# Scale and K in chunks of 4 and 5 k-tiles, with the ones put into PSUM ahead of them, in a diffusion transformer block

## The chip, the cores and the metric

The kernel runs on one core of a Trainium2 chip. The metric is the device time of one execution in microseconds (us). Six executions of the kernel before took 247.53 to 249.71 us, their median is 249.35 us. The profile is of one execution: its own time is 247.53 us, the lowest of the six, and the stretch that the profiler covers (the span) is 245.4 us of it. About 2.1 us lie around the span.

## The reference

The kernel computes one block of a diffusion transformer for 2 batches of 256 tokens, D = 1152, two heads, and a hidden layer of 4608. All inputs are bf16.

```
mod = (silu(c) @ w_mod).reshape(B, 6, 1, D)
shift_a, scale_a, gate_a, shift_m, scale_m, gate_m = mod[:, 0..5]
h   = layernorm(x) * (1 + scale_a) + shift_a
q, k, v = split(h @ wqkv)
a   = softmax(q @ k.T * Dh ** -0.5) @ v @ wo
x   = x + gate_a * a
h2  = layernorm(x) * (1 + scale_m) + shift_m
out = x + gate_m * (gelu(h2 @ w_fc1) @ w_fc2)
```

What matters here is the start: the normalised x is multiplied by `1 + scale_a`, and K is taken from that product before shift_a is added. The shift adds the same term to every key of a batch, so that it drops out of the softmax; Q and V are taken from the product with the shift.

## The kernel before

D is cut into nine tiles of 128 ("k-tiles"), the 512 tokens into four token tiles, two for each batch. The head of the kernel goes as follows.

1. SP's queue loads x (two DMAs, one for each batch), then the scale columns of w_mod (WSC) for the first KC = 5 k-tiles in three DMAs of 480 KB (line 699), then the first five row tiles of the K weights (WK, 288 KB each, line 702), then WSC for the other four k-tiles, the other four of WK, and then the shift columns (WSH, three DMAs of 864 KB, line 704). These loads wait for nothing. After them come the Q weights (WQ), which take WSC's place in SBUF and so wait until WSC has been read.
2. silu(c) is made on ScalarE and VectorE (lines 721 to 727), while TensorE runs 16 dummy matmuls of 512 columns (`warm_a`, line 716, and `warm`, line 773).
3. LayerNorm's statistics of token tiles 1 and 2 are taken on VectorE (`ln_stats_dve`), of 0 and 3 on ScalarE by two sums (`ln_stats_act`); the power of -1/2 is GpSimd's. VectorE normalises each tile (`xn_*`, line 756), TensorE transposes it into PSUM (`xn_T`, line 763).
4. TensorE makes scale_a as columns: for each of the k-tiles of the contraction and each output k-tile of the chunk one matmul with 2 columns (`mod_kt`, line 778), accumulated in bank 7. `sc1a` (line 784) adds 1 on the way from PSUM to SBUF. `hk` (line 789) multiplies a transposed k-tile by that column, which gives HK. For k-tiles of the first chunk it reads PSUM; the others are first copied to HX (`xn_T_copy`, line 769).
5. TensorE makes K for batch 0 (four pairs of output tiles, banks 0 to 3) and batch 1 (three pairs, banks 5, 4, 6) with `k_pair` (line 807), k-tile after k-tile: the first chunk's k-tiles for batch 0, one pair of chunk and batch 1, then scale for the second chunk (36 matmuls with 2 columns), then the rest.
6. TensorE makes shift_a as rows ("shr", line 879: nine k-tiles of the contraction, each with four matmuls side by side in the array, of 384, 256, 256 and 256 columns), the last K pairs, Q, attention and the rest of the block. From here on the order is not touched by the change.

The order is set so: every operation is put down as a unit with an engine, a duration, and its reads and writes (class `Sched`). TensorE and SP keep program order. For VectorE and ScalarE a list (`S.first`, line 910) fixes the order of the head; after it, and on GpSimd, a list scheduler (`schedule`, line 281) picks by its own durations, which include a model of the DMA. Waits follow from the reads and writes. PSUM is tracked by bank, so that two engines that read one bank take turns, and TensorE writes a bank again when all that read it are done.

Of the kernel before, what the change touches and what calls it, by code (L numbers as in the profile page):

```python
# [171 lines left out]
class Sched:  # L172
# [107 lines left out]

    def schedule(self, dma_bw=385.0, dma_issue=650.0, dma_lat0=900.0, dma_lat1=600.0, verbose=False):
        units = self.units
# [30 lines left out]
        for u in units:  # L313
            if ndeps[u.uid] == 0:
                avail_time[u.uid] = 0.0
                ready[u.eng].append((-u.bl, u.uid))
        eng_free = {e: 0.0 for e in ENGINES}
        dma_free = 0.0
# [7 lines left out]
        while scheduled < n:  # L326
            progressed = False
            for e in ENGINES:
# [18 lines left out]
                if u.dma_bytes > 0:  # L347
                    u.end = now + u.dur
                    if e == "sp":
                        xs = max(u.end + dma_lat0, dma_free)  # L350
                        dma_free = xs + u.dma_bytes / dma_bw
                        u.fin = dma_free + dma_lat1
                    else:
                        u.fin = u.end + 1500.0 + u.dma_bytes / (dma_bw * 0.5) + dma_lat1
                else:
                    u.end = now + u.dur
                    u.fin = u.end + u.lat
# [143 lines left out]
P = 128  # L501
# [10 lines left out]
F0 = 8  # L512
KC = 5
KG = 6
# [30 lines left out]
def build_kernel(nc, x, c, wqkv, wo, w_mod, w_fc1, w_fc2, out):  # L545
# [5 lines left out]
    with (  # L551
# [94 lines left out]
        NMR2 = sb(misc(16), 16, F32)  # L646
        NHALF = sb(misc(4), 4, F32)
        ST32 = sb(misc(72), 72, F32)
        GMS = sb(misc(288), 288, F32)
# [16 lines left out]
        def dma(dst, src, nbytes, name, is_out=False, eng="sp", run=4096):  # L666
            eff = 1.0 if run >= 4096 else (1.08 if run >= 2304 else (1.15 if run >= 1536 else (1.3 if run >= 1024 else 1.42)))
            return S.op(eng, 500.0 if eng == "sp" else 150.0, lambda e: e.dma_start(dst, src), reads=[src], writes=[dst],  # L668
                        name=name, dma_bytes=nbytes * eff, is_out=is_out)

        def dve(cost, fn, reads, writes, name):
            return S.op("dve", cost, fn, reads=reads, writes=writes, name=name)
# [18 lines left out]


        dma(CSB[0:18, :], c.rearrange("b (k p) -> (b k) p", p=P), 18 * 256, "ld_c", eng="act")
        for b in range(2):
            dma(X[:, 2 * b:2 * b + 2, :], xv[b], 2 * P * D * 2, "ld_x%d" % b)
        for (ka, kb) in ((0, KC), (KC, KT)):
# [16 lines left out]

        S.op("pool", 100, lambda e: e.memset(NHALF, -0.5), writes=[NHALF], name="nhalf")

        dve(600, lambda e: e.memset(Q4B, 0.0), [], [Q4B], "zq4b")
        for i in range(2):
            S.unit("pe", 430.0, "warm_a%d" % i)
            mm(ps32(5), IDENT, Q4B, True, True)
# [19 lines left out]

        def ln_stats_act(src, junk, mv_t, msq, rstd_t, tag):  # L740
            mean, var = mv_t[:, 0:1], mv_t[:, 1:2]
            act(1420, lambda e: e.activation(out=junk, in_=src, func=ACTF.Square, scale=D ** -0.5, accum_out=msq), [src], [junk, msq], "sq_" + tag)
            act(1420, lambda e: e.activation(out=junk, in_=src, func=ACTF.Identity, scale=1.0 / D, accum_out=mean), [src], [junk, mean], "sum_" + tag)
            dve(170, lambda e: e.scalar_tensor_tensor(out=var, in0=mean, scalar=mean, in1=msq, op0=ALU.mult, op1=ALU.subtract),
                [mean, msq], [var], "nvar_" + tag)
            dve(150, lambda e: e.tensor_scalar(out=var, in0=var, scalar1=-1.0, scalar2=EPS, op0=ALU.mult, op1=ALU.add), [var], [var], "veps_" + tag)
            pool(650, lambda e: e.tensor_tensor(out=rstd_t, in0=var, in1=NHALF, op=ALU.pow), [var, NHALF], [rstd_t], "rstd_" + tag)

        for t in range(4):
            xt, xn, mv, rs = X[:, t, :], XN[:, t, :], MV[:, t, :], RSTD[:, t:t + 1]  # L750
            if t in (1, 2):
                ln_stats_dve(xt, [X[:, t, i * CH:(i + 1) * CH] for i in range(NCH)], BN[:, t, :], mv, rs, "ln1_%d" % t)
            else:
                ln_stats_act(xt, xn, mv, SUMS[:, t:t + 1], rs, "ln1_%d" % t)
            m = MV[:, t, 0:1]
            dve(c_dve_fast(D), lambda e, xt=xt, xn=xn, m=m, rs=rs: e.tensor_scalar(out=xn, in0=xt, scalar1=m, scalar2=rs,
                                                                                 op0=ALU.subtract, op1=ALU.mult),
                [xt, m, rs], [xn], "xn_%d" % t)


        XB = [(4, 5, 6), (6, 4, 5)]

        def xn_T(t):
            b = t // 2
            S.unit("pe", KT * c_mm(128), "xnT_%d" % t)
            for kt in range(KT):
                tr(ps16(XB[b][kt // 4], (kt % 4) * 256 + (t % 2) * 128, 128), XN[:, t, kt * 128:(kt + 1) * 128], IDENT)

        def xn_T_copy(b, k0, k1, eng):
            src = ps16(XB[b][k0 // 4], (k0 % 4) * 256, (k1 - k0) * 256).rearrange("p (k t) -> p k t", k=k1 - k0)  # L770
            copy_on(eng, HX[:, k0:k1, b * 256:(b + 1) * 256], src, (k1 - k0) * 256, True, "xnT_cp%d_%d" % (b, k0))

        def warm(n, tag):
            for i in range(n):
                S.unit("pe", 215.0, "warm_%s_%d" % (tag, i))
                mm(ps32(2), IDENT, Q4B, True, True)

        def mod_kt(W, kt, col0, name, fs=(0, 9)):
            S.unit("pe", (fs[1] - fs[0]) * 27.0, name)
            for f in range(*fs):  # L780
                mm(ps32(7, col0 + f * 2, 2), W[:, kt, f * 128:(f + 1) * 128], ST[:, kt:18:9], kt == 0 and f == fs[0], kt == KT - 1,
                   skip_group_check=True)

        def sc1a(ka, kb):
            m, o = ps32(7, 2 * ka, 2 * (kb - ka)), SC1A[:, 2 * ka:2 * kb]
            dve(170, lambda e: e.tensor_scalar(out=o, in0=m, scalar1=1.0, scalar2=None, op0=ALU.add), [m], [o], "sc1a_%d" % ka)  # L786


        def hk(kt, b, eng="dve"):
            dst, s1 = HK[:, kt, b * 256:(b + 1) * 256], SC1A[:, kt * 2 + b:kt * 2 + b + 1]  # L790
            src = ps16(XB[b][kt // 4], (kt % 4) * 256, 256) if kt < KC else HX[:, kt, b * 256:(b + 1) * 256]
            if eng == "act":
                act(c_act(256, 1), lambda e: e.activation(out=dst, in_=src, func=ACTF.Copy, scale=s1), [src, s1], [dst], "hk_%d_%d" % (kt, b))
                return
            dve(256 if kt < KC else 200, lambda e: e.tensor_scalar(out=dst, in0=src, scalar1=s1, scalar2=None, op0=ALU.mult),  # L795
                [src, s1], [dst], "hk_%d_%d" % (kt, b))
# [6 lines left out]

        KB = [(0, 1, 2, 3), (5, 4, 6)]
        ev_rr = [0]
# [16 lines left out]

        warm(14, "b")
        xn_T(1)
        for kt in range(0, 3):
            mod_kt(WSC, kt, 0, "sca_%d" % kt, (0, KC))
        xn_T(0)
        for kt in range(3, 6):
            mod_kt(WSC, kt, 0, "sca_%d" % kt, (0, KC))
        for kt in range(6, 9):  # L830
            mod_kt(WSC, kt, 0, "sca_%d" % kt, (0, KC))
        sc1a(0, KC)
        for kt in range(KC):
            hk(kt, 0, "act" if kt in (2, 4) else "dve")
        xn_T_copy(0, 8, 9, "act")
        xn_T_copy(0, 5, 8, "act")
        for kt in range(KC):
            for i in range(4):
                k_pair((kt,), i, 0)
            if kt == 1:  # L840
                xn_T(2)
            if kt == 2:
                xn_T(3)
                xn_T_copy(1, 8, 9, "act")
                xn_T_copy(1, 5, 8, "act")
        for kt in range(KC):
            hk(kt, 1, "act" if kt == 2 else "dve")
        k_pair(range(KC), 0, 1)
        for kt in range(KT):
            mod_kt(WSC, kt, 0, "scb_%d" % kt, (KC, KT))  # L850
        sc1a(KC, KT)
        for kt in range(KC, KT):
            for b in range(2):
                hk(kt, b)
        k_pair(range(KC), 1, 1)
        k_pair(range(KC), 2, 1)
# [39 lines left out]
        for kt in range(KT):  # L896
            for b in range(2):
# [5 lines left out]
                else:  # L903
# [6 lines left out]
        S.first = {  # L910
            "dve": ["zq4b", "c_half", "c_silu", "bn_ln1_1_0", "bn_ln1_1_1", "bn_ln1_1_2", "aggr_ln1_1", "veps_ln1_1", "bn_ln1_2_0", "nvar_ln1_0", "veps_ln1_0",
                    "xn_1", "xn_0", "bn_ln1_2_1", "bn_ln1_2_2", "aggr_ln1_2", "veps_ln1_2", "nvar_ln1_3", "veps_ln1_3",
                    "sc1a_0", "hk_0_0", "xn_2", "hk_1_0", "xn_3", "hk_3_0", "hk_0_1", "hk_1_1", "hk_3_1", "hk_4_1", "sc1a_5"],
            "act": ["ld_c", "c_tanh", "sq_ln1_0", "sum_ln1_0", "sq_ln1_3", "sum_ln1_3", "xnT_cp0_8", "xnT_cp0_5", "hk_2_0", "hk_4_0",
                    "hk_2_1", "xnT_cp1_8", "xnT_cp1_5"],
        }
# [352 lines left out]
```

## Time and profile before

| of the profiled execution | |
|---|---|
| its own time | 247.53 us |
| span | 245.4 us |
| TensorE busy | 239.5 us (98%) |
| VectorE / ScalarE / GpSimd busy | 98.5 / 63.1 / 20.2 us |
| moved by DMA | 51.59 MB, mean 210 GB/s |
| first matmul of K starts | 12.11 us |
| first matmul of shr starts | 28.12 us |
| granted TensorE clock | 9 of 10 or more in all 40 slices |

A profile names a group of instructions by line, engine, operation and tiles; all of SBUF is one tensor, `arena`, and all of PSUM another, `psum`, and all matmuls are issued at line 687 (transposes at 690), so that stretches of the head are told apart by shape and time. PE is TensorE's matmuls, PEld its weight loads, DVE VectorE, ACT ScalarE, POOL GpSimd, SPq the DMA issue of SP. Times in the chain, the timeline and the table of stretches count from the start of the span.

### The profile page before, as it was taken

What the parts mean: (1) busy time and instruction counts of PE and PEld (TensorE: products, weight loads), DVE (VectorE), ACT (ScalarE), POOL (GpSimd) and SP (SyncE); (2) the same over time, 40 slices, a digit from 0 to 9 for tenths busy, and PEclk for the clock granted to TensorE, in tenths of its full rate; (3) what the DMA queues carried; (4) which work ended last, traced back from release to release, by engine and by line L of the source; (5) the groups of instructions that cost most, each with busy time, mean ns of one, the idle gap of its engine ahead of it and who ended that gap; (6) DMA issues with size and microseconds to landing.
All of it is one profiled execution on the core that took longest, in us unless ns stands there. A gap on an engine that the chain in (4) does not pass through costs nothing.

```text
span 245.4 us, 4021 instructions
## 1 busy us (share of the span) xinstructions
PE 239.5 (98%) x1753; PEld 147.2 (60%) x1753; DVE 98.5 (40%) x201; ACT 63.1 (26%) x127; POOL 20.2 (8%) x34
## 2 busy tenths in 40 slices
PE   7799999999999999999999999999999999999995
PEld 2488754556656756898544444444566656665674
DVE  3743450455313679869999600000022221111112
ACT  5630340244311305983322333222000000000000
POOL 1300000000011176600000000020000000000000
PEclk9999999999999999999999999999999999999999
DMA  7999999999993999979943488021000000000000
GB/s 244 352 377 391 392 390 408 418 419 405 382 305 91 329 382 392 392 259 400 348 132 101 170 295 330 0 54 46 0 16 19 16 16 20 16 16 28 22 16 19
DMA packets 28844, 51.59 MB, mean 210 GB/s; under 512 B 1559, under 2 KB 15643, under 8 KB 28827
## 3 DMA queue, kind: packets, MB, share of 16 engines
q1 hardware_dynamic: 28384, 50.14, 56.7%
q0 software_dynamic: 416, 1.19, 1.7%
q8 instruction: 14, 0.23, 0.4%
q14 instruction: 3, 0.02, 0.0%
q10 hardware_dynamic: 27, 0.00, 0.0%
HBM read 50.14 MB, written 1.19 MB: 209 GB/s over the span
## 4 chain that ended last, share of the span: by engine, by line
PE 94%; DMA 3%; SPq 1%; DVE 0%; issue 0%
PE psum L687 93%; DMA arena<-in_w_mod_dram 3%; PE psum L690 2%; SPq L668 1%; DVE arena L795 0%; DVE arena L1207 0%; DVE arena L1208 0%; DVE arena L786 0%
## 5 line engine op out<-in xcount | busy, mean ns | idle before, releaser
L687 PE MATMUL psum<-arena 128*128 128x384 bf16 (+11 forms) x1664 | 236.1, 310 | 2.9 <-POOL arena L710 1.4
L687 PEld LDWEIGHTS psum<-arena 128*128 128x128 bf16 (+3 forms) x1664 | 141.9, 97 | 92.8 <-issue 5.4
L1207 DVE TENSOR_TENSOR arena<-psum,arena 128x384 f32<-128x384 f32 (+3 forms) x14 | 7.0, 501 | 68.0 <-PE psum L687 68.0
L1117 ACT ACTIVATE arena<-psum 128x512 bf16<-128x512 f32 (+1 forms) x44 | 22.4, 520 | 42.7 <-PE psum L687 42.7
L684 DVE CAST arena<-psum 128x512 bf16<-128x512 f32 (+4 forms) x22 | 13.8, 633 | 31.8 <-PE psum L687 31.7
L682 ACT ACTIVATE arena<-psum 128x512 bf16<-128x512 f32 (+6 forms) x27 | 14.8, 563 | 35.0 <-PE psum L687 32.4
L1018 DVE SCALAR_TENSOR_TENSOR arena<-arena 128x1152 f32<-128x1152 bf16 x16 | 22.7, 1416 | 0.5
L1085 POOL TENSOR_TENSOR arena<-arena 128x384 f32<-128x384 f32 x12 | 10.9, 912 | 13.5 <-DVE arena L1084 11.3
L668 POOL DMA_DIRECT2D dit_scratch<-arena x3 | 1.8, 610 | 116.7 <-ACT arena L682 59.8
L734 DVE BATCH_NORM_STATS2 arena<-arena 128x6 f32<-128x384 f32 (+1 forms) x18 | 9.5, 549 | 1.0 <-DMA arena<-in_x_dram 0.9
L1030 DVE CAST arena<-psum 72x32 bf16<-72x32 f32 x1 | 0.2, 186 | 21.2 <-PE psum L687 21.2
L1084 DVE TENSOR_TENSOR arena<-psum,arena 128x384 f32<-128x384 f32 x12 | 6.7, 556 | 3.8 <-PE psum L687 3.8
L1090 ACT ACTIVATE arena<-arena 128x1152 bf16<-128x1152 f32 x4 | 5.3, 1343 | 9.8 <-DVE arena L1089 9.8
L1208 DVE TENSOR_TENSOR arena<-arena 128x384 bf16<-128x384 f32 (+3 forms) x14 | 7.0, 500 | 0.5
L690 PEld LDWEIGHTS psum<-arena 128*128 128x128 bf16 (+1 forms) x89 | 5.8, 98 | 2.3 <-DMA arena<-in_c_dram 0.8
L690 PE MATMUL psum<-arena 128*128 128x128 bf16 (+1 forms) x89 | 7.1, 219 | 0.0
L1107 ACT ACTIVATE arena<-psum,arena 128x128 bf16<-128x128 bf16 x16 | 6.1, 455 | 2.8 <-PE psum L690 2.2
L1104 DVE TENSOR_SCALAR arena<-psum,arena 128x128 bf16<-128x128 bf16 x20 | 5.5, 337 | 1.9 <-PE psum L690 1.9
L948 ACT ACTIVATE arena<-psum,arena 128x256 bf16<-128x256 f32 x8 | 3.7, 470 | 7.3 <-DVE arena L945 4.6
L738 POOL TENSOR_TENSOR arena<-arena 128x1 f32<-128x1 f32 x6 | 3.3, 553 | 7.7 <-DVE arena L737 7.7
L944 DVE TENSOR_REDUCE arena<-psum 128x2 f32<-128x512 f32 x4 | 2.8, 692 | 2.6 <-PE psum L687 2.6
L795 DVE TENSOR_SCALAR arena<-psum,arena 128x256 bf16<-128x256 bf16 x7 | 2.4, 349 | 3.6 <-PE psum L690 2.3
(43 smaller groups left out, 42.9 us busy)
## 6 DMA issues: line engine op xcount, KB each, us to landing
arena<-in_w_mod_dram SPq DMA_DIRECT2D x4, 2592.0 KB, 20.4
arena<-in_w_fc_dram SPq DMA_DIRECT2D x9, 1152.0 KB, 7.5
arena<-in_w_fc_dram SPq DMA_DIRECT2D x4, 2592.0 KB, 16.2
arena<-in_wqkv_dram SPq DMA_DIRECT2D x18, 288.0 KB, 10.2
arena<-in_w_mod_dram SPq DMA_DIRECT2D x3, 864.0 KB, 13.1
arena<-in_wqkv_dram SPq DMA_DIRECT2D x1, 2592.0 KB, 12.5
arena<-in_wo_dram SPq DMA_DIRECT2D x1, 2592.0 KB, 32.8
arena<-in_w_mod_dram SPq DMA_DIRECT2D x3, 480.0 KB, 7.3
```

What stands on the lines that cost most here:

```text
L682: act(c_act(n), lambda e: e.activation(out=dst, in_=src, func=ACTF.Copy), [src], [dst], name)
L684: dve(c_dve_psum16(n) if psum16 else c_dve_psum32(n), lambda e: e.tensor_copy(dst, src), [src], [dst], name)
L687: S.instr(lambda e: e.matmul(o, lhsT=l, rhs=r, start=st, stop=sp, **kw), reads=[l, r], writes=[o])
L690: S.instr(lambda e: e.transpose(o, i_, idn), reads=[i_, idn], writes=[o])
L734: dve(550, lambda e, s=s, o=o: e.bn_stats(out=o, in_=s), [s], [o], "bn_%s_%d" % (tag, ci))
L1018: dve(1270, lambda e, w=w, s=s, acc=acc: e.scalar_tensor_tensor(out=acc, in0=w, scalar=s, in1=acc, op0=ALU.mult, op1=ALU.add), [w, s, acc] ...
L1084: dve(550, lambda e, o=o, ga=ga, x1c=x1c: e.tensor_tensor(out=x1c, in0=o, in1=ga, op=ALU.mult), [o, ga], [x1c], "wo_t1_%d_%d" % (t, ci))
L1085: S.op("pool", 930, lambda e, xs=xs, x1c=x1c: e.tensor_tensor(out=x1c, in0=x1c, in1=xs, op=ALU.add), reads=[x1c, xs], writes=[x1c], name=" ...
L1107: act(440, lambda e, o=o, dst=dst, s1=s1, s2=s2: e.activation(out=dst, in_=o, func=ACTF.Identity, scale=s1, bias=s2), [o, s1, s2], [dst], ...
L1117: act(c_act(ntok), lambda e: e.activation(out=dst, in_=o, func=ACTF.Gelu_apprx_tanh), [o], [dst], "gelu_%d_%d" % (f, tok0))
L1207: dve(c_dve_psum32(w), lambda e, o=o, gm=gm, t1=t1: e.tensor_tensor(out=t1, in0=o, in1=gm, op=ALU.mult), [o, gm], [t1], "fc2_t1_%d_%d" % ( ...
L1208: dve(c_dve_32(w), lambda e, t1=t1, x1c=x1c, ost=ost: e.tensor_tensor(out=ost, in0=t1, in1=x1c, op=ALU.add), [t1, x1c], [ost], "fc2_out_%d ...
```

## The change

- KC is 4 instead of 5: the first chunk of scale and K has four k-tiles (three DMAs of 384 KB, then four of WK), the second five (three of 480 KB, then five of WK).
- The 1 of `1 + scale_a` is no longer added by `sc1a`. Before scale is accumulated, one matmul of the identity with a tile of ones (`sc_ones`) writes ones into bank 7, and all of `mod_kt`'s matmuls accumulate on top of it. `hk` of k-tile 0 and batch 0 takes its column straight from PSUM, ahead of `sc1a`, which is now a plain copy.
- x of batch 0 is loaded in two DMAs, one for each token tile.
- Of batch 1, the variance steps leave VectorE: for token tile 2, EPS is added on GpSimd; for tile 3, the mean's square less EPS is made on ScalarE (`mm_ln1_3`) and the subtraction on GpSimd.
- The transposes and scale's matmuls are ordered anew: tile 1's transposes, scale for contraction tiles 0 to 5, tile 0's transposes, scale for 6 to 8. Batch 1's transposes (tile 3, then 2) stand together after K's second k-tile, and go to banks 6, 5 and 7. Two pairs of batch 1, not one, stand ahead of the second chunk's scale, and batch 1's K banks are 4, 5, 6.
- Who multiplies is shared out anew: of the first chunk ScalarE takes k-tiles 2 and 3 of batch 0 alone, and copies four k-tiles where it copied three.
- Dummy matmuls: three at `warm_a`, then 2, 8 and 1 (the last one between scale and K), where there were 2 and 14.
- The scheduler's constants change (rates, latencies and durations of the units).

From shr on, all engines have the same instructions in the same order in both kernels; ahead of it, only what is listed here has moved.

```diff
-KC = 5
+KC = 4
-        for b in range(2):
-            dma(X[:, 2 * b:2 * b + 2, :], xv[b], 2 * P * D * 2, "ld_x%d" % b)
+        for t in range(2):
+            dma(X[:, t, :], xv[0][:, t, :], P * D * 2, "ld_x%d" % t, run=2304)
+        dma(X[:, 2:4, :], xv[1], 2 * P * D * 2, "ld_x23")
...
+            pool(250, lambda e: e.tensor_scalar(out=var, in0=var, scalar1=EPS, scalar2=1.0, op0=ALU.add, op1=ALU.mult), [var], [var], "veps_" + tag)
...
+                act(220, lambda e: e.activation(out=var, in_=mean, func=ACTF.Identity, scale=mean, bias=NEPS), [mean, NEPS], [var], "mm_" + tag)
+                pool(300, lambda e: e.tensor_tensor(out=var, in0=msq, in1=var, op=ALU.subtract), [msq, var], [var], "var_" + tag)
...
-        XB = [(4, 5, 6), (6, 4, 5)]
+        XB = [(4, 5, 6), (6, 5, 7)]
...
-                mm(ps32(7, col0 + f * 2, 2), W[:, kt, f * 128:(f + 1) * 128], ST[:, kt:18:9], kt == 0 and f == fs[0], kt == KT - 1,
-                   skip_group_check=True)
+                mm(ps32(7, col0 + f * 2, 2), W[:, kt, f * 128:(f + 1) * 128], ST[:, kt:18:9], False, kt == KT - 1, skip_group_check=True)
...
-            dve(170, lambda e: e.tensor_scalar(out=o, in0=m, scalar1=1.0, scalar2=None, op0=ALU.add), [m], [o], "sc1a_%d" % ka)
+            dve(180, lambda e: e.tensor_copy(o, m), [m], [o], "sc1a_%d" % ka)
...
+            s1 = ps32(7, 0, 1) if kt == 0 and b == 0 else SC1A[:, kt * 2 + b:kt * 2 + b + 1]
...
-        KB = [(0, 1, 2, 3), (5, 4, 6)]
+        KB = [(0, 1, 2, 3), (4, 5, 6)]
...
+        def sc_ones(ka, kb):
+            S.unit("pe", 60.0, "ones_%d" % ka)
+            mm(ps32(7, 2 * ka, 2 * (kb - ka)), IDENT, ONES[:, 2 * ka:2 * kb], True, True)
+
+        warm(2, "a")
+        sc_ones(0, KC)
+        warm(8, "b")
         xn_T(1)
+        sca(0, 6)
         xn_T(0)
+        sca(6, 9)
+        warm(1, "d")
+        hk(0, 0)
         sc1a(0, KC)
+        hk(1, 0)
         xn_T_copy(0, 8, 9, "act")
+        xn_T_copy(0, 4, 8, "act")
+        hk(2, 0, "act")
+        hk(3, 0, "act")
...
+        k_first(0)
+        k_first(1)
+        xn_T(3)
+        xn_T(2)
+        k_first(2)
+        xn_T_copy(1, 8, 9, "act")
+        xn_T_copy(1, 4, 8, "act")
         for kt in range(KC):
+            hk(kt, 1)
+        k_first(3)
         k_pair(range(KC), 0, 1)
+        k_pair(range(KC), 1, 1)
+        sc_ones(KC, KT)
         for kt in range(KT):
             mod_kt(WSC, kt, 0, "scb_%d" % kt, (KC, KT))
         sc1a(KC, KT)
```

## The prediction

> **What bounds the kernel now.** I read the page's first part, then its chain, because only work on the chain can move the end.
>
> ```profile
> PE 239.5 (98%) x1753; PEld 147.2 (60%) x1753; DVE 98.5 (40%) x201; ACT 63.1 (26%) x127; POOL 20.2 (8%) x34
> PE 94%; DMA 3%; SPq 1%; DVE 0%; issue 0%
> ```
>
> TensorE is busy for 98% of the span, and the chain is TensorE for 94%; the rest of the chain is a DMA at the start. A head-only change can gain no more than what lies ahead of the first K matmul. The chain in order of time shows that stretch:
>
> ```profile
> 2.69 8.06 DMA arena<-in_w_mod_dram
> 10.75 0.05 issue
> 10.80 0.67 PE psum L687 x15
> 11.47 0.02 issue
> 11.49 0.18 DVE arena L786
> 11.68 0.02 issue
> 11.70 0.36 DVE arena L795
> 12.06 0.05 issue
> 12.11 1.92 PE psum L687 x16
> ...
> 15.91 44.09 PE psum L687 x355
> ```
>
> The third scale load lands at 2.69 + 8.06 = 10.75; then come 15 scale matmuls (0.67), the added 1 (0.18), the first multiplied tile (0.36), and K at 12.11. From there TensorE never waits for long. But the chain names only the last releaser; a load that lands just in time does not show in it. So I looked up every load's landing in the DMA answers against its first reader. Most are early by microseconds (the Q weights' last part lands some 8 us ahead of its use); the second chunk's last scale load, at 19.2, is early by some 0.3, but is moved forward by the change. The one that is tight and stays is the third part of the shift columns, which shr reads:
>
> ```profile
> 14.91 1.41 SPq L668 DMA_DIRECT2D arena<-in_w_mod_dram  x1
> arena<-in_w_mod_dram SPq DMA_DIRECT2D x1, 864.0 KB, 14.0
> 28.12 1.84 PE L687 MATMUL psum<-arena 128*2 128x384 bf16 x35
> 29.68 0.11 PEld L687 LDWEIGHTS psum<-arena 128*128 128x128 bf16 x2 [0.33 <-issue]
> ```
>
> Issued at 14.91, it lands 14.0 later, at 28.9. shr starts at 28.12 and its successor at 29.68, so nine k-tiles take about 1.5, 0.16 each. Its seventh k-tile, the first that reads this load, is due at 28.12 + 6 x 0.16 = 29.1: only 0.2 after the landing. A start of shr more than 0.2 earlier meets an empty buffer. Can the load come sooner? Two stretches:
>
> ```profile
> 5.00:10.00 5.00, 5.00 (x57) 2.86 (x55) 4.25 (x12) 4.65 (x10) 1.38 (x2) 1.00 0.99 336
> 25.00:30.00 5.00, 5.00 (x69) 3.85 (x67) 2.19 (x4) 2.39 (x4) 0.00 (x0) 1.00 1.05 390
> ```
>
> The last columns are the DMA share and GB/s: the 16 DMA engines are full from the start until past 30. The bytes ahead of that landing (x 1152, scale 2592, WK 2592, shift 2592 KB) are the same after the change, only in another order.
>
> **What the Trainium skill says.** "TensorE: Matmul & The Clock Gate", section "What's actually happening": TensorE runs at half its clock until a window of about 3.4 us was busy, the windows run free of the kernel, and an idle window takes it back to half. The trace agrees on the first half: weight loads of the dummies stand 0.43 apart up to 6.75 and some 0.2 apart after 7.1; no falling back is in this trace. "Runtime: NRT & Kernel Launch", section "Instruction fetch mechanics": instructions are fetched in 16 KiB blocks by a DMA queue. The page's third part agrees: queue 8 moved 14 packets, 0.23 MB, in 0.4% of 16 engines' span, so 0.004 x 16 x 245.4 / 14 = 1.1 us of one engine each. "DMA: Bandwidth & Descriptors", section "Queues, rings and completion order": one DMA is split over rings of up to 16 engines, which share their time between queues. The trace fits: the second chunk's second and third scale loads were issued at 6.61 and 8.08 and landed 10.1 and 11.1 later, at 16.7 and 19.2, 2.5 apart where 384 KB at 376 GB/s need 1.05; one block was fetched between 16.0 and 17.2.
>
> **The change, part by part.**
>
> Scale's first chunk: three loads of 384 instead of 480 KB leave 288 KB (0.295 MB) out ahead of the last landing: at 370 GB/s 0.8 us. Shorter rows (1024 for 1280 bytes; x of batch 0 in rows of 2304 for 4608) could cost rate. Stretches with 1280-byte rows ran at 320 to 335 GB/s, one with 1024-byte rows (15 to 16 us) at 352, so below nothing is possible too; I take nothing, bounds -0.1 and +0.2. Landing at 10.0. Then 12 matmuls instead of 15 (0.67 - 3 x 0.034 = 0.57), no added 1 on the path (-0.20), and the multiply as before (0.36; its column now from PSUM, nearest row the same line at 0.35, bounds 0 to +0.1): 10.0 + 0.05 + 0.57 + 0.02 + 0.36 + 0.05 = 11.05. WK's first tile now lands where the third scale load did, 10.75 to 10.9, just ahead: covered by 0.15, and 0.1 later if the row sizes cost. The last dummy (0.22) runs under the multiply (0.43). **K starts about 1.0 earlier, at 11.1.**
>
> x by tile, LayerNorm: tile 0 lands about 0.29 MB / 0.39 = 0.75 before 4.35, so ScalarE's four sums (1.3 each) end at 8.7 instead of 9.3. Tile 0's transposes now stand behind the second scale load (about 9.0) and end near 10.0, hidden by the third load; without that cover 0.5. VectorE loses three steps of 0.15 to 0.21. ScalarE gains one (0.19 to 0.38, the reading of an accumulator and a 256-column copy; I take 0.25), with batch 0's copies and multiplies behind it; GpSimd gains two (0.1 to 0.57 each, its memset and its power), and rstd of tiles 3 and 2, queued behind them, come near 10.2 and 11.3. VectorE wants them at 11.7 and 12.3: covered by 1; uncovered, up to 1.1. The extra DMA issue on SP costs 0.4 ahead of scale loads that would wait for bandwidth anyway: nothing.
>
> ScalarE's copies and two multiplies: the four-tile copy by the row of three (0.81) about 1.05; chain 10.1 + 0.38 + 1.05 + 2 x 0.47 = 12.5, wanted at 11.1 + 16 x 0.11 + 18 x 0.056 = 13.9. Covered by 1.4. VectorE's four multiplies of batch 1 start at 13.9 and end at 15.3, wanted from 14.8 one by one: covered, at worst 0.3. The ones for the second chunk wait for ScalarE's copy out of bank 7, near 14.5, and are due at 17.3; queued behind them is all of TensorE, but there are 2.8 of cover.
>
> Second chunk of scale: nine more 2-column matmuls and the ones, 10 x 0.034 = +0.35 on TensorE. Its last load ends 288 KB earlier than the second chunk's did, at 18.4 instead of 19.16; TensorE wants it at 11.1 + 48 x 0.11 + 1.0 + 1.1 = 18.4. A wait of 0 to 0.4; I take 0.15.
>
> The path to shr: 28.12 - 1.0 + 0.35 + 0.15 = 27.6. Its seventh k-tile is due at 27.6 + 1.0 = 28.6, but the load lands at 28.9: TensorE waits 0.3, and the rest follows from 28.95 instead of 29.1. **Of 1.0 gained at K, 0.5 is given back in the head, 0.3 in a new wait, and 0.15 stays.** With the landing 0.1 later nothing stays; with it 0.5 earlier, where no instruction block meets a late DMA engine, 0.5. I take 0.25 for the middle. In the profiled execution: 245.4 - 0.25 + 2.1 = 247.3. That execution is 1.8 below the median, and the page does not say why; applied to the median: 249.35 - 0.25 = **249.1 us**. Case 1, within 0.8 either side.
>
> **The rivals.** R1, all of the head counts. Five of six executions are 1.5 to 2.2 longer than the profiled one. If they lose it on TensorE, because K starts at half clock after the quiet stretch from 7.9 to 12.1 (one window of 3.4 at half rate costs 1.7), then the shift columns are long there when shr comes, and the shorter quiet stretch with its extra dummy saves that loss. Against it: nothing in this trace shows a fall of the clock; for it, the size. Gain 1.7 + 0.15, less some: 247.8.
>
> R2, slower by the clock. Despite its name the change has fewer dummies: 13 ahead of the first transposes, not 16. At 0.43 they end near 7.1, and tile 1's normalised values come at 7.7. A window that starts in 6.6 to 7.8 then sees almost only transposes and 2-column matmuls, and K starts at half rate: +1.7, arriving at shr at 29.3, 1.2 past today's 28.12: 250.5. It decides from a loss above 0.5 on. Against it: the same quiet stretch, longer, is in the kernel before.
>
> R3, the late DMA engine. Shr hangs on the slowest engine; if both blocks fetched by 26 hit it, 28.9 becomes 30.0 and the end +0.9: 250.2. Against it: the bytes are the same, and so it could as well be better.
>
> That the change does not do what it says can be excluded for its order, not for its effect: the K start could stay at WK's first load (11.5 today), which still leaves case 1.
>
> **How the numbers follow.** Case 1 has 0.57, R1 0.23, R2 0.12, R3 0.08. About 0.5% (1.25 us) is what a measurement of this kernel can tell from no change. Faster by more than that: most of R1, 0.21. Slower by more: half of R2 and R3 and a stall unforeseen, 0.14. Same 0.65. The range runs from R1 to R2: 247.7 to 250.6, and leaves out about 0.15.
>
> **What would show it.** K's first 256-column matmul near 11.1; scale's third load landing near 10.0; the fourth k-tile's matmuls and the second scale without a gap over 0.4; shr starting near 27.6, a wait of TensorE for the w_mod load at 28.9, and shr's successor near 29.5. Wrong would be: a landing of the shift columns away from 28.9 by over 0.5; shr starting after 28.1; 256-column matmuls 0.21 apart instead of 0.11 after the start of K; or a profile like this one and yet a median lower by 1 us.

## The result and the profile after

The changed kernel takes 249.88 us (median of 31 executions, 248.41 to 250.84), the kernel before beside it 248.40 us (68 executions, 246.98 to 249.95). The ratio is 1.0057, with a 95% interval of 1.0041 to 1.0073: slower by 0.6%, where 0.1% faster was forecast. Ratios are those on record, over the executions that count as fast, and are not the quotient of the two medians.

The profiled execution of the changed kernel took 248.59 us, its span is 246.9 us; before these were 247.53 and 245.4. First the page's busy times and the shares of the chain, as for the kernel before.

```profile
PE 239.0 (97%) x1753; PEld 147.3 (60%) x1753; DVE 98.1 (40%) x199; ACT 63.7 (26%) x127; POOL 21.0 (9%) x37
...
PE 95%; DMA 3%; DVE 1%; SPq 0%; issue 0%
```

The loss isn't visible here: TensorE has as many instructions and 0.5 us less of busy time. The chain in order of time (start, us, what) shows the head:

```profile
1.70 6.34 DMA arena<-in_x_dram
8.04 0.02 issue
8.06 0.56 DVE arena L746
8.62 0.13 DVE arena L757
8.76 0.02 issue
8.78 0.15 DVE arena L759
8.93 0.50 DVE arena L773
9.43 0.05 issue
9.48 0.68 PE psum L691 x9
10.15 0.61 PE psum L688 x24
10.77 0.52 PE psum L691 x9
11.29 0.49 PE psum L688 x12
11.78 0.03 issue
11.81 0.37 DVE arena L816
12.18 0.05 issue
12.22 3.14 PE psum L688 x16
```

Read it from the top. What releases the head is no longer a load of scale but the third load of x, that of batch 1. It lands at 1.70 + 6.34 = 8.04; before, where x came in two loads, it landed at 5.78. VectorE's queue has a statistics step of this batch (L746) ahead of tile 1's steps, so that tile 1 is normalised only from 8.93 to 9.43; its transposes (L691 x9) start at 9.48, before at 7.88. The scale matmuls follow at once (24, then 12), and K starts at 12.22, where 11.1 was forecast and 12.11 was measured before. The last line is the larger loss: K's first 16 matmuls take 3.14 us, before 1.92, 0.21 apart where they stood 0.11 apart. The stretches say why (columns: length, then busy us and count of PE, PEld, DVE, ACT, POOL, then the granted TensorE clock, the DMA share and GB/s):

```profile
6.00:7.00 1.00, 0.05 (x1) 0.00 (x0) 0.39 (x2) 0.37 (x2) 0.48 (x1) 1.00 0.75 224
7.00:8.00 1.00, 0.00 (x0) 0.00 (x0) 0.00 (x0) 0.00 (x0) 0.09 (x1) 1.00 1.01 303
...
11.00:12.00 1.00, 1.00 (x19) 0.54 (x16) 0.80 (x3) 0.70 (x3) 0.74 (x2) 0.67 1.01 393
12.00:13.00 1.00, 0.92 (x5) 0.58 (x5) 0.96 (x4) 0.97 (x2) 0.90 (x2) 0.50 1.04 398
13.00:14.00 1.00, 1.00 (x7) 0.70 (x5) 0.69 (x2) 0.50 (x2) 0.14 (x1) 0.50 1.06 390
14.00:15.00 1.00, 1.00 (x8) 0.73 (x7) 0.00 (x0) 0.00 (x0) 0.00 (x0) 0.62 1.07 369
```

TensorE does nothing from 6.05 to 9.48. A clock of 0.67 in the slice from 11 means full until 11.34 and half after it; 0.62 in the slice from 14 means full again from 14.75. So one stretch of 3.41 us ran at half the clock, and K started inside it. The same two slices before:

```profile
12.00:13.00 1.00, 0.89 (x9) 0.81 (x10) 1.00 (x4) 0.17 (x1) 0.00 (x0) 1.00 1.02 387
13.00:14.00 1.00, 1.00 (x13) 0.91 (x11) 0.64 (x2) 0.67 (x2) 0.00 (x0) 1.00 1.05 390
```

The end of the head in the changed kernel:

```profile
29.76 1.95 PE L688 MATMUL psum<-arena 128*2 128x384 bf16 x38
31.31 1.75 PEld L688 LDWEIGHTS psum<-arena 128*128 128x128 bf16 x17 [0.33 <-issue]
```

Shr starts at 29.76 instead of 28.12, and what follows it at 31.32 instead of 29.68: +1.64. From there to the end of the span it is 215.54 us, before 215.72. The whole difference is in the head.

**One profile doesn't tell a median.** Each execution's record gives its mean granted clock. One window of 3.41 us at half the clock lowers it by 0.5 x 3.41 / 247 = 0.007, so that 1.000 to 0.996 means no window lost, 0.995 to 0.991 one, 0.989 and below two. The executions of the kernel before beside the experiments below, and those of the changed kernel, its profiled one among them, sorted so (median us, number):

| | none lost | one | two |
|---|---|---|---|
| before (201) | 247.51 (72) | 249.06 (119) | 250.47 (10) |
| changed (32) | none | 248.78 (9) | 250.12 (23) |

A lost window costs 1.3 to 1.55 us. In the three profiles below that lost two (e4, e6, e9) the two follow each other: one fall of the clock that lasts 6.8 us. The kernel before loses one in 59% of its executions and two in 5%; its profile, with a clock of 1.000, is one of the 36% that lose none. The changed kernel always loses one, and in 72% two; its profile is of the better kind. Weighted by these shares the two come to 248.57 and 249.74. On average the changed kernel loses 1.72 windows, the kernel before 0.69: one window more, about as long as the 1.4 us (0.57%) between the two. At an equal number of lost windows the medians of the changed kernel are 0.3 us lower, which so few executions don't tell from nothing.

### The profile page after: what moved, and what is told of

Its sections match the earlier page's. It is cut to its first block, busy times and chain, and to the rows that moved or that the text cites. A ratio compares the mean times of both kernels' runs of the same rounds, so it can differ in the third digit from the quotient of the medians.

```text
span 246.9 us, 4025 instructions
## 1 busy us (share of the span) xinstructions
PE 239.0 (97%) x1753; PEld 147.3 (60%) x1753; DVE 98.1 (40%) x199; ACT 63.7 (26%) x127; POOL 21.0 (9%) x37
## 4 chain that ended last, share of the span: by engine, by line
PE 95%; DMA 3%; DVE 1%; SPq 0%; issue 0%
PE psum L688 93%; DMA arena<-in_x_dram 3%; PE psum L691 2%; SPq L669 0%; DVE arena L816 0%; DVE arena L746 0%; DVE arena L773 0%; DVE arena L1242 0%; DVE arena L1243 0%; DVE arena L806 0%; DVE arena L759 0%; DVE arena L757 0%
## 5 line engine op out<-in xcount | busy, mean ns | idle before, releaser
L691 PE MATMUL psum<-arena 128*128 128x128 bf16 (+1 forms) x89 | 6.9, 219 | 3.4 <-DVE arena L773 3.4
L691 PEld LDWEIGHTS psum<-arena 128*128 128x128 bf16 (+1 forms) x89 | 5.7, 98 | 5.6 <-DVE arena L773 3.9
L737 DVE BATCH_NORM_STATS2 arena<-arena 128x6 f32<-128x384 f32 (+1 forms) x15 | 7.9, 549 | 0.8 <-DMA arena<-in_x_dram 0.7
L936 ACT ACTIVATE arena<-arena 128x256 bf16<-128x256 bf16 x6 | 2.5, 496 | 3.8 <-DVE arena L930 3.8
L741 POOL TENSOR_TENSOR arena<-arena 128x1 f32<-128x1 f32 x5 | 2.8, 556 | 5.8 <-DVE arena L740 5.8
```

The costliest lines, as they stand in the source:

```text
L691: S.instr(lambda e: e.transpose(o, i_, idn), reads=[i_, idn], writes=[o])
L737: dve(550, lambda e, s=s, o=o: e.bn_stats(out=o, in_=s), [s], [o], "bn_%s_%d" % (tag, ci))
```

## The experiments

The theory: the quiet stretch of TensorE ahead of K, in which it does nothing or only transposes and 2-column matmuls, costs a window of the clock, and two parts of the change lengthen it: three dummies fewer at its start, and the third load of x, late, in its middle. The rivals: the third load of x costs by what waits for it and the clock is a side show; or VectorE's order, not the load, makes the wait; or the end is set by the shift columns whatever happens in the head. No kernel here leaves out a part of the computation.

### What makes the quiet stretch

**e1**, the changed kernel with eight dummies more:

```diff
-        warm(8, "b")
+        warm(16, "b")
         xn_T(1)
```

> The changed kernel with 16 dummy matmuls instead of 8 ahead of tile 1's transposes. Theory 'clock' (the dummies end too early, TensorE is quiet for a window of 3.4 us and K starts at half rate): no fall of the granted clock in this run's profile, the first 16 K matmuls take 1.75 us instead of 3.14, and the median falls from 249.9 to 248.0 to 248.5 us. Theory 'late x' (x of batch 1 lands at 8.0 instead of 5.8 and holds VectorE's queue): no gain, K still starts at 12.2; 249.9. Theory 'shift load' (shr waits for a load that lands at 30.1): gain of at most 0.5, and TensorE waits in shr.

Measured: 248.83 us against 248.73 before, ratio 1.0006 (0.9987 to 1.0025). Thirteen of 22 executions lose no window, eight one, one two. That is a little more than the 248.0 to 248.5 expected, and the profile, expected to keep the clock, lost a window. In it the dummies run to 8.25, x of batch 1 still lands late (7.67) and K starts at 12.49. So the ratio falls by 0.005 (1.3 us) with dummies alone, while K starts later than in either kernel.

**e2**, the changed kernel with x of batch 0 in one load, as before:

```diff
-        for t in range(2):
-            dma(X[:, t, :], xv[0][:, t, :], P * D * 2, "ld_x%d" % t, run=2304)
-        dma(X[:, 2:4, :], xv[1], 2 * P * D * 2, "ld_x23")
+        for b in range(2):
+            dma(X[:, 2 * b:2 * b + 2, :], xv[b], 2 * P * D * 2, "ld_x%d" % b)
```

> The changed kernel with x of batch 0 in one load, as before the change. Theory 'late x': x of batch 1 lands near 5.8 again, tile 1's transposes start near 7.6 instead of 9.5, the quiet stretch of TensorE shrinks from 3.4 to 1.6 us, K starts near 11.1; if the clock falls all the same, the median is 249.4, if not, 248.0. If the late landing has nothing to do with the split, x of batch 1 lands at 7 to 8 here too and the median stays at 249.9. Theory 'clock' alone expects the fall also here, in most executions, since the dummies are as few.

Measured: 248.22 us against 248.73, ratio 0.9995 (0.9971 to 1.0019); five of 14 executions lose no window, seven one, two two. The chain of its profile:

```profile
2.15 7.09 DMA arena<-in_w_mod_dram
...
9.76 0.90 PE psum L691 x9
...
11.70 0.82 PE psum L688 x3
```

The chain is led by a scale load again, and K starts at 11.70, half a microsecond ahead of the changed kernel. The profile itself lost a window (9.74 to 13.15, hence 0.90 for nine transposes that take 0.52 to 0.68 in the changed kernel). Each of the two repairs alone brings the time back to that of the kernel before; each also shifts the shares of lost windows by about one class.

**e4**, the kernel before with six dummies fewer, for the first suspect alone:

```diff
-        warm(14, "b")
+        warm(8, "b")
         xn_T(1)
```

> The kernel before with 8 dummy matmuls instead of 14 ahead of tile 1's transposes, nothing else. Theory 'clock': the kernel before has two groups of times, near 247.6 and near 249.3, and the upper one is a fall of the clock ahead of K; with fewer dummies nearly all executions fall, and the median moves from 248.4 to 249.3 or above. Theories 'late x' and 'shift load': the dummies end before tile 1 is ready in both, nothing moves, 248.4.

Measured: 249.67 us, ratio 1.0054 (1.0033 to 1.0074). Sixteen of 22 executions lost two windows or three (fourteen and two; their median is 249.39). Its profile runs at half clock from 9.10 to 15.92, two windows; two of the slices:

```profile
12.00:13.00 1.00, 0.98 (x5) 0.72 (x6) 1.00 (x3) 0.26 (x1) 0.00 (x0) 0.50 1.04 406
...
14.00:15.00 1.00, 1.00 (x7) 0.67 (x6) 0.00 (x0) 0.00 (x0) 0.00 (x0) 0.50 1.11 365
```

Fewer dummies alone are enough to make the kernel before as slow as the changed one. Six executions show a clock of 1.000 and yet a median of 250.25. The record counts the clock as full until it is first released (in the profile of before it shows 1.00 from 5 to 10, while the dummies' weight loads stand 0.43 apart up to 6.75), so that a release that comes only after K's start would look like that. This was not shown.

**e3**, the changed kernel with VectorE's first step on batch 1 put behind the normalising of tiles 1 and 0:

```diff
-            ... "aggr_ln1_1", "veps_ln1_1", "bn_ln1_2_0",
-                    "nvar_ln1_0", "veps_ln1_0", "xn_1", "xn_0", "bn_ln1_2_1", ...
+            ... "aggr_ln1_1", "veps_ln1_1",
+                    "nvar_ln1_0", "veps_ln1_0", "xn_1", "xn_0", "bn_ln1_2_0", "bn_ln1_2_1", ...
```

> The changed kernel with VectorE's first statistics step of tile 2 moved behind the normalising of tiles 1 and 0, so that x of batch 1, however late, doesn't hold tile 1. Theory 'late x': tile 1's transposes start near 7.7 instead of 9.5 whatever the landing of x of batch 1; K starts where scale's third load lets it, 11.8 to 12.0 if that lands at 11.2 as in the changed kernel; gain 0.3. Theory 'clock': the quiet stretch ahead of the transposes is 1.6 us, but the one after them is as long as before; the clock still falls in most executions; 249.5 to 249.9.

Measured: 249.68 us, ratio 1.0047 (1.0029 to 1.0064), hardly better than the changed kernel's 1.0057. No execution kept the clock; twelve lost one window, ten two. The chain of its profile:

```profile
2.64 7.72 DMA arena<-in_w_mod_dram
...
10.88 0.98 PE psum L691 x9
...
12.72 0.39 PE psum L688
```

The wait for VectorE is gone (tile 1's transposes start at 7.59, not 9.48), and nothing is won: the window from 7.18 to 10.59, with those transposes and a few scale matmuls in it, still loses the clock (tile 0's transposes take 0.98), and the scale loads behind x are as late as in the changed kernel (the second at 10.36, the third at 11.44). The order on VectorE explains the 3.4 us wait that the changed kernel's waits show, but not its time. This rival falls.

### What the lost windows are worth

**e5**, the kernel before with five dummies inside the quiet stretch, behind tile 1's transposes and behind scale:

```diff
         xn_T(1)
+        warm(3, "c")
         for kt in range(0, 3):
...
             mod_kt(WSC, kt, 0, "sca_%d" % kt, (0, KC))
+        warm(2, "d")
         sc1a(0, KC)
```

> The kernel before with three dummy matmuls more behind tile 1's transposes and two behind scale's first chunk, under the multiply. Theory 'clock': two thirds of the executions of the kernel before lose one window at half rate in K (248.9 against 247.4); with the quiet stretch filled nearly all keep the full clock, and the median moves from 248.7 to 247.5. Theory 'the two groups have another cause, and the mean clock only goes with it': two groups stay, median 248.7.

Measured: 247.39 us against 248.94, ratio 0.9961 (0.9940 to 0.9983). Nineteen of 22 executions lose no window, and three one; beside it the kernel before lost at least one in 48 of 75. Its profile:

```profile
12.00:13.00 1.00, 0.70 (x8) 0.61 (x8) 1.00 (x4) 0.00 (x0) 0.00 (x0) 1.00 1.07 416
...
14.00:15.00 1.00, 1.00 (x16) 0.95 (x14) 0.00 (x0) 0.00 (x0) 0.00 (x0) 1.00 1.09 358
```

K starts at 12.33 in it, 0.2 later than in the profile of before, and the median is 1.55 us lower. The loss in most executions of the kernel before was the clock, and five dummies end it. No other run is told apart from it as faster, and the edit is of two lines.

**e7**, the changed kernel with the quiet stretch filled and x of batch 0 in one load (the edit of e2), so that what remains of the change can be read at full clock:

```diff
-        warm(8, "b")
+        warm(12, "b")
         xn_T(1)
-        sca(0, 6)
+        sca(0, 3)
+        warm(3, "c")
+        sca(3, 6)
         xn_T(0)
+        warm(2, "e")
         sca(6, 9)
-        warm(1, "d")
+        warm(2, "d")
```

> The changed kernel with x of batch 0 in one load, 12 dummies instead of 8, and further dummies between the scale groups (3), behind tile 0's transposes (2) and under the first multiply (2 instead of 1). Theory 'clock' with 'late x': full clock in nearly all executions, K starts at 11.7, the median is 247.0 to 247.3, at or a little below the full-clock group of the kernel before (247.4). Theory 'shift load': TensorE then reaches shr near 28 and waits there for the load, which lands at 28.9 to 29.4, so that of the 0.4 won at K's start 0.2 at most are left.

Measured: 248.15 us against 248.94, ratio 0.9973 (0.9952 to 0.9993). All 22 executions keep the clock. Yet the median is above the 247.0 to 247.3 expected if only the clock and the late x counted, and 0.6 us above the executions of the kernel before that keep it (247.53 there, 27 executions), though K starts at 11.67. What is late shows in its waits (engine, line, waited for: us in total, times, longest) and in its chain:

```profile
PE psum L688 <- DMA arena<-in_w_mod_dram: 0.3, 1, 0.3
```

```profile
14.66 14.74 DMA arena<-in_w_mod_dram
29.40 0.04 issue
29.44 1.63 PE psum L688 x19
```

Shr starts at 27.99, TensorE waits for the third load of the shift columns, which lands at 29.40, and shr's successor starts at 30.03, 0.35 later than before. That is the wait that the forecast named, with a landing half a microsecond later than it had.

It is not all of the 0.6. In e7's profile the last matmul ends 0.35 later than before (242.77 against 242.42), but the span is 1.2 longer: the rest lies at the very end. SP issues the last store of the output only when all stores but the one just ahead of it have landed, and one of them is late (size and us from issue to landing, then SP's wait for it):

```profile
out_dram<-arena SPq DMA_DIRECT2D x1, 56.0 KB, 3.5
SPq L471 <- DMA out_dram<-arena: 1.6, 1, 1.6
```

Before, this store took 1.5 us. In e7 a block of instructions (queue 8) is fetched from 242.24 to 243.54, and eight of the store's packets start only from 243.52 on, the others by 242.21. The profiles of e10, e11 and e12 show the same (3.0 to 3.2 us); in the two kernels and in e8 the store takes 1.5, and in e8 the fetch begins at 241.81, just behind the start of the store's last packet (241.75). The added dummies move the fetch against the store; no run tests that by itself, nor how many executions it meets.

**e8**, e7 with five of the nine k-tiles of the K pair behind shr put ahead of it, so that shr comes later and the load is there:

```diff
+        k_pair(range(5), 3, 1, bank=1)
         sh_split = ((0, 3), (3, 5), (5, 7), (7, 9))
...
-        k_pair(range(KT), 3, 1, bank=1)
+        k_pair(range(5, KT), 3, 1, bank=1)
```

> As e7, with the last K pair of batch 1 cut in two, ten matmuls (1.1 us) ahead of shr and eight behind it, so that shr asks for the shift columns 1.1 us later with the same work done. Theory 'shift load': the wait in shr goes, and the median is 0.2 to 0.6 below e7. If shr didn't wait in e7, nothing moves (within 0.1), or it is longer by up to 0.3, where shr's copy out of PSUM is no longer covered by the 18 matmuls.

Measured: 247.51 us, ratio 0.9972 (0.9951 to 0.9994); beside e7 on the same chip the median is 0.64 us less and the mean 0.42, though the two ratios, 0.9973 and 0.9972, don't tell the runs apart. All executions keep the clock. The slice around the landing, in e7 and then in e8:

```profile
29.00:29.50 0.50, 0.19 (x5) 0.06 (x8) 0.00 (x0) 0.00 (x0) 0.00 (x0) 1.00 1.05 392
```

```profile
29.00:29.50 0.50, 0.50 (x17) 0.38 (x19) 0.00 (x0) 0.00 (x0) 0.00 (x0) 1.00 1.08 401
```

TensorE is busy for 0.19 of 0.50 us in e7, and for all of it in e8. So the shift columns do bound the head at full clock: without the wait, the last matmul ends 0.46 earlier than in e7 (242.31 against 242.77). The other 1.2 between the two spans (246.6 and 245.0) is the store at the end, so that the medians are no clean measure of the wait. The changed order now reaches the 247.5 that the kernel before has whenever it keeps its clock, and no more.

### The third load of x

**e6**, the kernel before with x of batch 0 in two loads, one for each token tile:

```diff
-        for b in range(2):
-            dma(X[:, 2 * b:2 * b + 2, :], xv[b], 2 * P * D * 2, "ld_x%d" % b)
+        for t in range(2):
+            dma(X[:, t, :], xv[0][:, t, :], P * D * 2, "ld_x%d" % t, run=2304)
+        dma(X[:, 2:4, :], xv[1], 2 * P * D * 2, "ld_x23")
```

> The kernel before with x of batch 0 in two loads, nothing else of the change. Theory 'late x': x of batch 1 lands at 7.6 to 8.0 instead of 5.8, tile 1's transposes move from 7.9 to 9.3, the dummies (14) leave a longer quiet stretch, so that nearly all executions lose a window: 249.3 to 250. If the late landing in the changed kernel comes from the smaller scale loads behind it, x of batch 1 lands at 5.8 here and the median stays at 248.7.

Measured: 250.66 us against 248.94, ratio 1.0080 (1.0057 to 1.0104). That is above the 249.3 to 250 expected. One of 22 executions keeps the clock, nine lose one window, twelve two. x lands at 3.57, 4.25 and 8.06, and the chain is:

```profile
3.15 8.82 DMA arena<-in_w_mod_dram
11.97 0.05 issue
12.02 0.68 PE psum L687 x15
...
13.34 0.82 PE psum L687 x3
```

The third scale load lands 1.2 later than before, and K starts 1.2 later, besides the clock. This single part of the change costs at least as much as the whole.

**e9**, the same with x of batch 0 cut by partitions, 64 each, so that each row is as long as before:

```diff
+        for h in range(2):
+            dma(X[64 * h:64 * h + 64, 0:2, :], xv[0][64 * h:64 * h + 64], P * D * 2, "ld_x%d" % h)
+        dma(X[:, 2:4, :], xv[1], 2 * P * D * 2, "ld_x23")
```

> The kernel before with x of batch 0 in two loads of 64 partitions each, so that the rows stay 4608 bytes long and only the number of loads is that of the changed kernel. If the rows of 2304 bytes make x of batch 1 late, it lands near 5.8 here; if it is the third load in flight, it lands at 7.6 to 8.1 as in the changed kernel. Only the landing is read.

Measured, in one execution: 251.5 us, and x of batch 1 lands at 8.89. The DMA answers for that load (KB, us from issue to landing) of the kernel before and of e9:

```profile
arena<-in_x_dram SPq DMA_DIRECT2D x1, 576.0 KB, 4.5
```

```profile
arena<-in_x_dram SPq DMA_DIRECT2D x1, 576.0 KB, 6.8
```

The same bytes in the same rows take 2.3 us longer. By this one execution row length is not the reason; that there are three loads in place of two fits all runs. Why a third load should cost so much stays open. Its landing is counted in 16 steps of a semaphore: in the changed kernel 13 come by 6.50 and the last at 8.04, before all within 5.39 to 5.78, so that a few late parts hold VectorE.

**e11**, e7 with x by token tile again:

```diff
-        for b in range(2):
-            dma(X[:, 2 * b:2 * b + 2, :], xv[b], 2 * P * D * 2, "ld_x%d" % b)
+        for t in range(2):
+            dma(X[:, t, :], xv[0][:, t, :], P * D * 2, "ld_x%d" % t, run=2304)
+        dma(X[:, 2:4, :], xv[1], 2 * P * D * 2, "ld_x23")
```

> As e7, but with x of batch 0 split as in the changed kernel: the changed kernel with the quiet stretches filled and nothing else. Theory 'clock' alone: all executions at full clock and 247.2 to 248.2, like e7. Theory 'late x': x of batch 1 at 7.6 to 8.1, tile 1's transposes at 9.3, longer than the dummies reach, so that part of the executions still fall; those at full clock take 0.3 to 0.8 more than e7, 248.2 to 249.

Measured: 249.21 us, ratio 1.0011 (0.9991 to 1.0030); all 20 executions keep the clock, where a part was expected to fall. Against e7's 248.15 the split costs 1.06 us at full clock (on another chip; the ratios differ by 0.0038, or 0.9 us). Not all of it is the split's own price: x of batch 1 lands at 8.53, the transposes wait until 9.96, and the dummies behind them, which in e7 filled waiting time, now stand in the path for about 1.1 us. The two could not be separated.

### The smaller scale loads

**e10**, e7 with scale loaded in chunks of 5 + 4 k-tiles, as before, and still computed in 4 + 5:

```diff
+            la, lb = (0, KC + 1) if ka == 0 else (KC + 1, KT)
-            w = (kb - ka) * P
+            w = (lb - la) * P
```

> As e7, but with scale loaded as before the change (five k-tiles, then four) and computed in chunks of 4 and 5. If scale's first loads take their time by bytes, its third load lands 0.8 later than in e7 (11.4 instead of 10.6) and K starts 0.8 later. If the row size sets it (1280 bytes for 1024), it lands at 10.7 and K starts within 0.2 of e7: then the smaller chunk brought next to nothing at K's start. By the theory 'shift load' the median stays within 0.3 of e7 either way.

Measured: 248.19 us against 249.00, ratio 0.9983 (0.9960 to 1.0006); all 20 executions keep the clock. The third scale load in e7 and in e10 (KB, us from issue to landing):

```profile
arena<-in_w_mod_dram SPq DMA_DIRECT2D x1, 384.0 KB, 7.9
```

```profile
arena<-in_w_mod_dram SPq DMA_DIRECT2D x1, 480.0 KB, 7.8
```

Issued at 2.70 and 2.73, they land at 10.62 and 10.55. Leaving 288 KB out ahead of this landing brings nothing that shows. The first of the three does land earlier with 384 KB (7.61 against 8.06); by the third that is gone. Why is open. The shift columns land at 28.63 here and shr doesn't wait; it starts 0.3 later than in e7, but its successor 0.2 earlier (29.83), and the last matmul ends 0.2 earlier (242.57). So the head doesn't explain that the medians of the two, from two chips, are the same; the late store at the end is in both profiles.

**e12**, e10 with e8's split of the K pair:

```diff
+            la, lb = (0, KC + 1) if ka == 0 else (KC + 1, KT)
...
+        k_pair(range(5), 3, 1, bank=1)
...
-        k_pair(range(KT), 3, 1, bank=1)
+        k_pair(range(5, KT), 3, 1, bank=1)
```

> e10 with the last K pair cut as in e8: x of batch 0 whole, scale loaded as before and computed in chunks of 4 and 5, the quiet stretches filled, ten K matmuls ahead of shr. By the theory 'shift load' the cut takes 0.3 to 0.7 off e10's 248.2, and all executions keep the full clock: 247.2 to 247.8, below both kernels. If e10's time above the full-clock group of the kernel before (247.5) has another cause than shr, nothing moves and it stays at 248.2.

Measured: 247.70 us against 248.62, ratio 0.9965 (0.9938 to 0.9991); all 15 executions keep the clock. It is not told apart from e5 (0.9961) and e8 (0.9972). All three beat both kernels, and e5 does it with the order of the kernel before.

## Why the prediction was wrong

What failed is the landing of scale (step 1), the time of tile 1's values (step 5) and, deciding the sign, the clock, which case 1 has at nothing in its sum (step 6). By its own steps:

1. "Landing at 10.0", from 288 KB less at 370 GB/s. It failed: 11.17 in the changed kernel. The term was mis-sized twice. The smaller loads were to be worth 0.8 and are worth nothing that shows: 10.62 in e7 and 10.55 in e10, where before it was 10.75. And splitting x, whose extra issue on SP was to cost "nothing", adds some 0.55 to the changed kernel (11.17 against e2's 10.63). In the kernel before it adds 1.2 (e6).

2. From that landing to K, 1.05. Right to the hundredth: 12.22 - 11.17 = 1.05 in the changed kernel, and 11.67 - 10.62 = 1.05 in e7, against 12.11 - 10.75 = 1.36 before. The ones in PSUM and three matmuls fewer do bring 0.3.

3. From K to shr, 16.5. Right at full clock: 27.99 - 11.67 = 16.32 in e7, before 16.01. (Its 11.1 + 48 x 0.11 + 1.0 + 1.1 is 18.5, not 18.4; that takes 0.1 off a wait.) In the changed kernel it took 17.54, so that of the 1.64 at shr some 1.22 are the half clock, 0.31 the longer way and 0.11 the later K.

4. Shr waits 0.3 for the shift columns. Right in its mechanism (e7, and e8, which takes it away), with the landing too early: 28.9 was taken, and it was 29.40 in e7 and 30.11 in the changed kernel. The 0.15 that should have stayed is thereby a loss of 0.35 at shr's successor. The prediction had put it beside the sum, "with the landing 0.1 later nothing stays"; that the bytes ahead of the landing are the same was no ground for the same landing.

5. "Tile 1's normalised values come at 7.7." It failed: 9.43, since the step of batch 1 ahead of them on VectorE waited for the third load of x. The order on that queue was known; that the load behind the split would land 2.3 later was not.

6. The clock. This decided the sign. R2 described what happened: dummies that end too early (at 6.05, sooner even than its 7.1), a window with hardly more than transposes, K at half rate, shr at 29.76. It was given 0.12 for the reason that "the same quiet stretch, longer, is in the kernel before". That reason holds of one profile with its clock at 1.000; in 64% of its executions the kernel before does lose a window. R1's premise, that five of six executions lost their 1.5 to 2.2 us on TensorE at K's start, was thus most likely right: e5 shows such a loss in most executions of the kernel before, though for those six, but the profiled one, no clock is on record. Its conclusion, that the change saves that loss, was wrong: 13 dummies in place of 16, a quiet stretch that begins earlier and a last dummy of 0.2 us give the windows more room, not less. The two rivals were two ends of one mechanism and should have been weighed together: most executions near the edge, and a change that moves TensorE's activity away from the edge or across it.

The section "What's actually happening" of "TensorE: Matmul & The Clock Gate" in the Trainium skill states free-running windows of 3.4 us, one of which, when idle, takes the clock to half. The trace agrees with the length (11.34 to 14.75) and with the free running (the same kernel loses none, one or two). But the lost windows were not idle: in each of the seven profiles with a fall, the window ahead of it held at least nine transposes. The section states no measure of how much work keeps a window. Count only matmuls of 256 columns or more, at the 0.11 us (256) and 0.22 us (512) that they stand apart. Then a window from 7.0 to 10.4 with some 0.8 us of them, and 18 transposes, kept the clock (the kernel before); one from 6.3 to 9.7 with some 0.5 lost it (e2), one from 9.2 to 12.6 with 0.35 (e1), and one from 7.9 to 11.3 with none and 18 transposes (the changed kernel). All 14 profiles agree: windows at full clock up to K's start that kept it held 0.8 or more, those that lost it 0.5 or less. What transposes and 2-column matmuls count for, the runs don't show.

Of the other rivals: R3, shift columns later by a slow DMA engine, had the right size (30.11), and the trace fits it: 15 of the 16 steps in which that landing is counted come by 28.82, only the last at 30.11, after a block of instructions fetched from 26.85 to 27.95. No run tests it. At half clock the load costs nothing, since shr arrives at 29.76 and asks for it at 30.7; at full clock it is the 0.35 of step 4.

## What to carry to other kernels

Where executions of one kernel differ by a fixed amount, sort them by their mean granted clock before reading any single profile: a profile with its clock at 1.000 can hide what most executions lose. A stretch of a few microseconds in which TensorE does only transposes and tiny matmuls is to be priced at a half-clock window, weighted by the chance that one falls there, and a few dummies inside the stretch, where TensorE waits anyway, are the cheap remedy. A load split at the very start delayed those behind it here; look at who waits for the last of them, on each engine's queue, before counting the gain of the first. And read the end of the trace too: dummies in the head can move what happens there.

## What the runs showed of the hardware that was not expected

- A window lost costs 1.3 to 1.55 us of 247.5, and both kernels fall into groups by it (247.5, 249.1, 250.5 before). Windows of 3.41 us that kept the clock held at least some 0.8 us of matmuls of 256 columns or more, those that lost it at most some 0.5.
- x (1152 KB) in two loads has landed by 5.6 to 6.0 us of the span (before, e2, e5, e7, e10, e12); in three loads by 7.7 to 8.9 (changed, e1, e3, e6, e9, e11).
- In the head, three scale loads of 384 KB landed no earlier than three of 480 KB (10.62 and 10.55).
- The third load of the shift columns, 864 KB, took 14.0 us from its issue before and 14.7 in the changed kernel, with the same bytes ahead of it; it landed from 28.6 (e4, e5, e10) to 30.4 (e3).
- A store of 56 KB that took 1.5 us elsewhere took 3.0 to 3.5 in the four profiles (e7, e10, e11, e12) in which eight of its packets started only as the fetch of an instruction block ended.
